# Storing the expert results from ScalarE's queue instead of SyncE's

## The chip, the cores and the metric

The kernel runs on one core of a Trainium2 chip. The metric is the device time of one execution in microseconds. The engines are TensorE (PE; its weight loads are PEld), VectorE (DVE), ScalarE (ACT), GpSimd (POOL) and SyncE (SP). SP computes nothing; its queue issues DMA transfers. In the profile a name such as L1021 is a line of the kernel, and `out<-in` are tile names with the buffer numbers left out.

## What is computed

Pooled attention for 4 batches and 8 heads, and on its result one feed-forward layer (the "experts" of the code) with an ELU between two matrix products:

```python
q_pool = q.reshape(B, H, S // 2, 2, D).mean(axis=3)        # (4, 8, 576, 64)
scores = scale * np.matmul(q_pool, k.transpose(0, 1, 3, 2)) # (4, 8, 576, 1152)
attn = softmax(scores)
x = np.matmul(attn, v)            # rearranged to (2304, 512)
h = x @ w_in                      # (2304, 2048)
g = np.where(h > 0, h, np.exp(np.minimum(h, 0)) - 1)
return g @ w_out                  # (2304, 512), float32
```

## The kernel before

Each batch is a unit of 576 pooled query rows. Inside a unit the heads go in four pairs, and each pair in nine steps of 128 query rows (the last step takes 64 rows of both heads). Every float32 operand is split into a high and a low float16 part, and products are summed from three terms.

One attention step is a fixed chain over engines: PE makes the scores (lines 721 and 730); DVE reads them from PSUM, scales them and finds the row maximum (line 736); ACT takes the exponential (line 742) and the row sum (line 747); DVE takes its reciprocal (line 750); ACT or POOL writes the high part of the probabilities (lines 761 and 753); DVE writes the low part (line 756); a transposing DMA from SP's queue turns `ep` into `pT` (line 780); PE multiplies it with v (lines 819 and 825); ACT and DVE join the two parts (lines 837 and 842). There are three `ep` buffers, so DVE's line 736 of a later step must wait until the transpose of the step three before has read its buffer.

The experts of a unit come in two groups of 256 and 320 rows and are interleaved with the attention of the next unit. The first product is line 933, with lines 941, 944, 949, 954, 968 and 972 behind it; the second is line 1000. Its result is evicted per tile of 128 rows by ACT (`oe`, line 1011) from PSUM into a `tmp` buffer in SBUF. The last tile of a unit has 64 rows only, whose two halves ACT (line 1013) and then DVE (line 1014) add. Then `od` (line 1021) stores the tile to `out`. That makes five stores a unit, 20 in all: 16 of 256 KB and four of 128 KB.

A planner written in Python sets the order of everything. Each piece of work is a task with an engine, an expected duration, a key and the tasks it depends on. The planner runs a clock over five engines, "DMA" among them, and whenever one is free it starts the ready task with the smallest key. `emit` then writes the tasks' instructions in the order in which the planner started them, so each engine's queue has a fixed order, and a queue does not pass an instruction that waits. A store is a DMA task that depends on its eviction; the planner's clock starts it when its DMA engine comes to it, which may be well after the eviction:

```python
toe = plan.add("ACT", 605.0, pos[0] - CFG["KO"], oe, [prev, txd2], [op, ot, us])
plan.add("DMA", Move(480.0, 480.0), pos[0], od, [toe], [ot])
```

All 372 transfers of the program before are issued from SP's queue: loads of q, k, v and the weights, the small copies of `qT`, the transposes and the stores. Completion is counted on eight semaphores, used in turn.

Of the kernel before, what the change touches and what calls it, by code (L numbers as in the profile page):

```python
# [226 lines left out]
def attention_moe_kernel(  # L227
# [9 lines left out]
    nc = tc.nc  # L237
# [131 lines left out]
    def w_out16(g):  # L369
        return w_out[g // 2].ap[:, 2 * (g % 2):2 * (g % 2) + 2]  # L370
# [485 lines left out]
    def experts(u, gi, t0, t1):  # L856
# [5 lines left out]
        def step(cost):  # L862
            at = pos[0]
            pos[0] += (t1 - t0) * cost / total
            return at
# [51 lines left out]
        if True:  # L917
# [72 lines left out]
            for o in range(0, n, 128):  # L990
                tn = min(128, n - o)
                op, ot = plan.buf("r"), plan.buf("tmp")
                prev = None
                for qd in range(4):
                    def m2(qd=qd, o=o, tn=tn, gt=gt, op=op):
                        for i12 in range(12):
                            fi, (a, e) = i12 // 3, ((0, 0), (0, 1), (1, 0))[i12 % 3]
                            f, i = qd * 4 + fi, qd * 12 + i12
                            r0 = 0 if tn == 128 else 64 * (i % 2)
                            nc.tensor.matmul(  # L1000
                                op.ap[r0:r0 + tn, :], gt[qd].ap[:, a, fi, o:o + tn], w_out16(f // 2)[:, e, f % 2, :],
                                start=(i < 128 // tn), stop=(i >= 48 - 128 // tn), skip_group_check=(tn < 128),
                            )

                    c = 12 * (216.0 if tn == 128 else 110.0)
                    deps = gdone[qd] + w_done[1][2 * qd] + w_done[1][2 * qd + 1] + [prev]
                    prev = plan.add("PE", c, step(c), m2, deps, [op, gt[qd], w_out[qd]])

                def oe(o=o, tn=tn, op=op, ot=ot):
                    if tn == 128:  # L1010
                        nc.scalar.activation(out=ot.ap, in_=op.ap, func=AF.Copy, scale=us.ap[:, 4:5])
                    else:
                        nc.scalar.activation(out=ot.ap[0:64], in_=op.ap[64:128], func=AF.Copy, scale=us.ap[0:64, 4:5])
                        nc.vector.scalar_tensor_tensor(
                            out=ot.ap[0:64], in0=op.ap[0:64], scalar=us.ap[0:64, 4:5], in1=ot.ap[0:64],
                            op0=ALU.mult, op1=ALU.add,
                        )

                def od(o=o, tn=tn, ot=ot, g0=g0):
                    r0 = u.b * SQ + u.s0 + g0 + o  # L1020
                    nc.sync.dma_start(out=out[r0:r0 + tn, :], in_=ot.ap[0:tn])  # L1021

                toe = plan.add("ACT", 605.0, pos[0] - CFG["KO"], oe, [prev, txd2], [op, ot, us])
                plan.add("DMA", Move(480.0, 480.0), pos[0], od, [toe], [ot])

    for u in units:
# [37 lines left out]
```

## Time and profile before

| | us |
|---|---|
| runs shown, median of 3 | 947.41 |
| runs shown, lowest and highest | 945.33, 953.8 |
| profiled execution, device time | 947.0 |
| profiled execution, span from the first to the last instruction | 945.2 |

The profile is one execution. A row of the timeline gives the start, the time taken, the engine (with a q when it is the engine's queue that issues or waits), the line, the operation, the tiles, how many instructions were merged, and in brackets how long the engine had stood idle and what ended that. Times are counted from the span's start. Issues of DMA transfers and waits on semaphores are work of a queue and don't count as busy time of an engine.

### The profile page before, as it was taken

The numbers are of one execution on the slowest core, as the hardware profiler recorded it, in microseconds if no ns is written. First come the engines' busy times: TensorE is split into PE (matmuls) and PEld (weight loads), VectorE is DVE, ScalarE is ACT, GpSimd is POOL, SyncE is SP. The second block draws the span as 40 slices with busy tenths as digits, with TensorE's granted clock in tenths as the row PEclk, the third lists the DMA queues.
The fourth block names the chain that finished last, engine by engine and source line by source line (L and its number), as shares of the span: only waits on it lengthen the run. The fifth ranks groups of instructions, "written<-read, shape, count | busy, mean of one in ns | idle before, by whom it ended". The sixth has DMA issues, their size and how long they took to land.

```text
span 945.2 us, 14736 instructions
## 1 busy us (share of the span) xinstructions
PE 740.6 (78%) x5283; PEld 420.6 (44%) x5283; DVE 728.4 (77%) x1235; ACT 691.2 (73%) x1169; POOL 370.6 (39%) x344
## 2 busy tenths in 40 slices
PE   0256555566939898988997989769979899789997
PEld 0123232233716455445644544338436544366563
DVE  5998999989898878867785897877877897785220
ACT  4587868878778879767777997568877987675360
POOL 3420513101737757402623772226324852034260
PEclk9998656657959999999998989989989999789999
DMA  7899999999948679897598989886799889754000
GB/s 235 221 211 199 232 224 250 237 188 263 224 95 182 133 166 207 153 185 125 110 186 183 196 172 208 160 160 105 158 212 202 170 157 173 133 100 76 23 1 28
DMA packets 434056, 156.94 MB, mean 166 GB/s; under 512 B 395840, under 2 KB 414272, under 8 KB 433984
## 3 DMA queue, kind: packets, MB, share of 16 engines
q1 hardware_dynamic: 433984, 156.01, 79.6%
q8 instruction: 41, 0.67, 0.3%
q14 instruction: 31, 0.25, 0.1%
HBM read 45.09 MB, written 4.72 MB: 53 GB/s over the span
## 4 chain that ended last, share of the span: by engine, by line
PE 28%; DVE 17%; DMA 14%; ACT 7%; issue 6%; POOL 5%; SPq 1%; DVEq 0%; POOLq 0%; ACTq 0%
DMA pT<-ep 11%; PE r L933 11%; PE r L1000 9%; DVE ep L736 6%; DVE ep L756 5%; PE r L819 3%; ACT ep L742 3%; PE s L721 2%; PE r L825 2%; POOL g L972 2%; PE s L730 1%; DMA kT<-kn 1%; DVE x L842 1%; ACT ep L761 1%; ACT tmp L944 1%
## 5 line engine op out<-in xcount | busy, mean ns | idle before, releaser
L756 DVE SCALAR_TENSOR_TENSOR ep<-ep,nm 128x1152 f16<-128x1152 f32 x132 | 209.7, 1593 | 18.1 <-ACT ep L761 10.5
L742 ACT ACTIVATE ep<-ep,nm 128x1152 f32<-128x1152 f32 x132 | 165.2, 1251 | 77.4 <-DVE ep L736 57.9
L736 DVE TENSOR_SCALAR_CACHE_REDUCE ep<-s,sm 128x1152 f32<-128x1152 f32 x132 | 186.3, 1411 | 40.6 <-DMA pT<-ep 25.7
L933 PE MATMUL r<-x,wi 128*128 128x256 f16 (+1 forms) x1536 | 204.1, 293 | 8.1 <-DVE x L842 4.2
L721 PE MATMUL s<-kT,qT 128*128 128x512 f16 (+3 forms) x480 | 108.8, 368 | 90.8 <-DVE ep L736 71.3
L933 PEld LDWEIGHTS <-wi 128*128 128x128 f16 x1536 | 150.5, 100 | 58.4 <-issue 18.3
L1000 PE MATMUL r<-wo,g 128*128 128x512 f16 (+1 forms) x864 | 174.4, 380 | 0.0
L761 ACT ACTIVATE ep<-ep,nm 128x1152 f16<-128x1152 f32 x111 | 138.3, 1247 | 23.7 <-DVE nm L750 23.3
L819 PE MATMUL r<-pT,v 128*128 128x256 f16 (+1 forms) x855 | 107.3, 281 | 31.1 <-DMA pT<-ep 16.5
L1000 PEld LDWEIGHTS <-g 128*128 128x128 f16 (+1 forms) x864 | 73.1, 100 | 87.9 <-issue 9.3
L949 POOL TENSOR_SCALAR tmp<-tmp,us 128x320 f32<-128x320 f32 (+1 forms) x96 | 73.2, 765 | 93.3 <-ACT tmp L944 92.9
L721 PEld LDWEIGHTS <-qT 128*128 128x128 f16 (+1 forms) x480 | 40.8, 105 | 144.5 <-issue 113.6
L819 PEld LDWEIGHTS <-v 128*128 128x128 f16 x864 | 72.5, 108 | 62.6 <-issue 33.1
L954 DVE SCALAR_TENSOR_TENSOR tmp<-r,wk,tmp 128x320 f32<-128x320 f32 (+1 forms) x96 | 57.5, 611 | 31.0 <-POOL tmp L949 30.6
L753 POOL TENSOR_SCALAR ep<-ep,nm 128x1152 f16<-128x1152 f32 x21 | 29.2, 1392 | 128.7 <-DVE nm L750 127.3
L972 POOL TENSOR_TENSOR g<-tmp,g 128x320 f16<-128x320 f32 (+1 forms) x70 | 72.1, 1036 | 12.0 <-ACT g L968 10.4
L730 PE MATMUL s<-kT,qT 64*128 64x512 f16 (+3 forms) x480 | 72.2, 369 | 0.0
L825 PE MATMUL r<-pT,v 128*64 128x256 f16 (+1 forms) x855 | 67.6, 282 | 0.0
L384 POOL TENSOR_SCALAR q<-q,sm 128x576 f32<-128x576 f32 x14 | 12.6, 897 | 134.6 <-ACT qn L429 119.2
L941 ACT ACTIVATE tmp<-r 128x320 f32<-128x320 f32 (+1 forms) x96 | 46.5, 485 | 24.4 <-PE r L933 19.6
L944 ACT ACTIVATE tmp<-tmp,us 128x320 f32<-128x320 f32 (+1 forms) x96 | 58.0, 608 | 1.3
L837 ACT ACTIVATE x<-r,sm 64x256 f32<-64x256 f32 (+1 forms) x96 | 39.8, 414 | 23.7 <-PE r L825 22.3
(123 smaller groups left out, 960.1 us busy)
## 6 DMA issues: line engine op xcount, KB each, us to landing
k<-in_k_dram SPq DMA_DIRECT2D x16, 576.0 KB, 5.0
v<-in_v_dram SPq DMA_DIRECT2D x16, 576.0 KB, 4.6
q<-in_q_dram SPq DMA_DIRECT2D x32, 256.0 KB, 3.4
qT<-qT SPq DMA_DIRECT2D x48, 144.0 KB, 2.8
g<-in_moe_w_in_dram SPq DMA_DIRECT2D x13, 512.0 KB, 5.6
g<-in_moe_w_out_dram SPq DMA_DIRECT2D x13, 512.0 KB, 5.2
out_dram<-tmp SPq DMA_DIRECT2D x16, 256.0 KB, 2.8
pT<-ep SPq DMA_TRANSPOSE x130, 4.8
```

What stands on the lines that cost most here:

```text
L721: nc.tensor.matmul(s.ap[rows, c, 0:n], pr.qT.ap[:, 0, j, rows], keys[h][c], start=True, stop=False, skip_group_check=True,)
L730: nc.tensor.matmul(s.ap[rows, c, 0:n], pr.qT.ap[r, 1, j, rows], keys[h][c][r], start=False, stop=True, skip_group_check=True,)
L736: nc.vector.tensor_scalar(e_(), s.ap.rearrange("p a b -> p (a b)")[:, 0:S], pr.sm.ap[:, 12:13], None, op0=ALU.mult, op1=ALU.min, accum_out ...
L742: nc.scalar.activation(out=e_(), in_=e_(), func=AF.Exp, bias=nm.ap[:, 0:1], scale=-1.0, accum_out=nm.ap[:, 2:3],)
L756: nc.vector.scalar_tensor_tensor(out=p_(1), in0=e_(), scalar=nm.ap[:, 3:4], in1=p_(0), op0=ALU.mult, op1=ALU.subtract)
L761: nc.scalar.activation(out=p_(0), in_=e_(), func=AF.Copy, scale=nm.ap[:, 3:4])
L819: nc.tensor.matmul(x.ap[:, os], vt[:, order[c]].rearrange("p e d -> p (e d)"), pT.ap[:, c, cs], start=(c == 0), stop=False, skip_group_che ...
L825: nc.tensor.matmul(x.ap[r0:r0 + 64, os], vt[:, order[c], 0], pT.ap[:, NCH + c, cs], start=False, stop=(c >= NCH - 2), skip_group_check=True,)
L933: nc.tensor.matmul(hp.ap[:, f * n:(f + 1) * n], w[:, a, c, (f0 + f) * 128:(f0 + f + 1) * 128], x16.ap[:, e, c, g0:g0 + n], start=(i == 0), ...
L949: nc.gpsimd.tensor_scalar(en.ap[:, :m], en.ap[:, :m], -1.0, us.ap[:, 5:6], op0=ALU.add, op1=ALU.mult)
L972: nc.gpsimd.tensor_tensor(out=l, in0=gv, in1=h, op=ALU.subtract)
L1000: nc.tensor.matmul(op.ap[r0:r0 + tn, :], gt[qd].ap[:, a, fi, o:o + tn], w_out16(f // 2)[:, e, f % 2, :], start=(i < 128 // tn), stop=(i >= ...
```

## The change

The function `od` issues the store from ScalarE's queue. The planner's tasks, keys and durations are the same, so the order in which instructions are emitted is the same too; the 20 stores leave SP's order and stand in ACT's order, at the place where they were emitted.

```diff
                 def od(o=o, tn=tn, ot=ot, g0=g0):
                     r0 = u.b * SQ + u.s0 + g0 + o
-                    nc.sync.dma_start(out=out[r0:r0 + tn, :], in_=ot.ap[0:tn])
+                    nc.scalar.dma_start(out=out[r0:r0 + tn, :], in_=ot.ap[0:tn])

                 toe = plan.add("ACT", 605.0, pos[0] - CFG["KO"], oe, [prev, txd2], [op, ot, us])
                 plan.add("DMA", Move(480.0, 480.0), pos[0], od, [toe], [ot])
```

## Rows read from the trace of the kernel before

**Rows 1.** The page, busy time, share and instructions of each engine.

```profile
PE 740.6 (78%) x5283; PEld 420.6 (44%) x5283; DVE 728.4 (77%) x1235; ACT 691.2 (73%) x1169; POOL 370.6 (39%) x344
```

**Rows 2.** The page, the chain that ended last: shares of the span by line.

```profile
DMA pT<-ep 11%; PE r L933 11%; PE r L1000 9%; DVE ep L736 6%; DVE ep L756 5%; PE r L819 3%; ACT ep L742 3%; PE s L721 2%; PE r L825 2%; POOL g L972 2%; PE s L730 1%; DMA kT<-kn 1%; DVE x L842 1%; ACT ep L761 1%; ACT tmp L944 1%
```

**Rows 3.** Line 1021: issue in ns (min/median/max), first and last start.

```profile
L1021 SPq DMA_DIRECT2D out_dram<-tmp x20: 332/536/1487, 338.2 to 941.8; - x20
```

**Rows 4.** SP's own waits: who waited for whom, total us, times, longest us.

```profile
SPq L1021 <- ACT tmp L1011: 69.1, 4, 44.9
```

**Rows 5.** Timeline of SP, 860 to the end.

```profile
858.51 7.06 SPq L780 DMA_TRANSPOSE pT<-ep  x2
879.54 62.74 SPq L1021 DMA_DIRECT2D out_dram<-tmp  x5
```

**Rows 6.** Line 780, the same view; then who waited for its landing (us, times).

```profile
L780 SPq DMA_TRANSPOSE pT<-ep x130: 2382/2846/5228, 52.5 to 862.7; - x130
...
  DVE ep L736: 26.2, 27
...
DMA to landing us min/median/max: 4.5/4.9/10.1
```

**Rows 7.** Timeline of SP around three stores of the body.

```profile
405.12 1.49 SPq L1021 DMA_DIRECT2D out_dram<-tmp  x1
406.71 3.31 SPq L780 DMA_TRANSPOSE pT<-ep  x1
...
581.91 4.10 SPq L780 DMA_TRANSPOSE pT<-ep  x1
586.06 0.57 SPq L1021 DMA_DIRECT2D out_dram<-tmp  x1
586.74 7.08 SPq L780 DMA_TRANSPOSE pT<-ep  x2
...
798.34 0.35 SPq L1021 DMA_DIRECT2D out_dram<-tmp  x1
798.81 7.54 SPq L780 DMA_TRANSPOSE pT<-ep  x2
```

**Rows 8.** Timeline of DVE, 576 to 594: the reader behind the store at 586.06.

```profile
592.33 1.42 DVE L736 TENSOR_SCALAR_CACHE_REDUCE ep<-s,sm 128x1152 f32<-128x1152 f32 x1 [0.93 <-DMA pT<-ep]
```

**Rows 9.** Line 1011 from 339 to 341: ACT's queue; ns, then first and last start.

```profile
L1011 ACTq EVENT_SEMAPHORE  x1: 17/17/17, 340.0 to 340.0; - x1
```

**Rows 10.** Timeline of ACT at four places where a store is emitted.

```profile
337.49 0.67 ACT L1011 ACTIVATE tmp<-r,us 128x512 f32<-128x512 f32 x1
...
339.36 1.25 ACT L742 ACTIVATE ep<-ep,nm 128x1152 f32<-128x1152 f32 x1 [1.02 <-DVE ep L736]
...
584.43 1.25 ACT L742 ACTIVATE ep<-ep,nm 128x1152 f32<-128x1152 f32 x1
...
586.08 1.16 ACT L424 ACTIVATE kn<-v 128x1152 f16<-128x1152 f32 x1 [0.31 <-DMA v<-in_v_dram]
...
616.78 0.29 ACT L747 ACTIVATE nm<-nm,wk 128x1 f32<-128x1 f32 x1
617.47 1.26 ACT L742 ACTIVATE ep<-ep,nm 128x1152 f32<-128x1152 f32 x1 [0.39 <-DVE ep L736]
...
620.01 1.25 ACT L742 ACTIVATE ep<-ep,nm 128x1152 f32<-128x1152 f32 x1 [0.87 <-DVE ep L736]
...
809.64 0.69 ACT L1013 ACTIVATE tmp<-r,us 64x512 f32<-64x512 f32 x1 [0.43 <-PE r L1000]
811.61 1.26 ACT L742 ACTIVATE ep<-ep,nm 128x1152 f32<-128x1152 f32 x1 [1.28 <-DVE ep L736]
...
812.99 0.29 ACT L747 ACTIVATE nm<-nm,wk 128x1 f32<-128x1 f32 x1
```

**Rows 11.** Timeline of DVE, 807 to 817: the 64-row tile and line 747's reader.

```profile
811.49 0.74 DVE L1014 SCALAR_TENSOR_TENSOR tmp<-r,us,tmp 64x512 f32<-64x512 f32 x1
...
815.01 0.16 DVE L750 RECIPROCAL nm<-nm 128x1 f32<-128x1 f32 x1
```

## The prediction

> **What bounds the kernel now.** I read the busy shares first: PE 78%, DVE 77%, ACT 73% of the span [rows 1]. No engine is full, so what counts is who waits for whom. The chain that ended last says the same: its largest single item, 11%, is the transposing transfer `pT<-ep` (line 780), and the next are matmuls and the two big DVE passes [rows 2]. All those transfers are issued from SP's queue, in the order in which the planner wrote them, and the 20 stores of line 1021 stand in the same queue.
>
> So the question has two halves: what does SP's queue lose to the stores, and what will ACT's queue lose to them? A store occupies SP for 0.332 to 1.487 us, median 0.536 [rows 3]. The view of SP's own waits gives the largest number that speaks for the change: SP stood 69.1 us at line 1021 for the eviction of line 1011 [rows 4]. But it counts four waits, the longest 44.9 us, and the timeline of SP's end shows where they are: from 879.54 to the end SP holds five stores and nothing else [rows 5]. The transposes end before that. Nothing stands behind these waits, so removing them is worth nothing.
>
> **What is removed from SP.** Fifteen stores lie in the body (338 to 813 us), five in the tail. A body store delays something only where the next transfer was ready and had to go behind it. That is so in six spots; the first is 405.12 to 406.71 (1.59 us), the last 798.34 to 798.81 (0.47) [rows 7]; the four between them are 0.70, 0.71, 2.16 (two stores together) and 0.68. In sum 6.3 us of SP's time. In the other spots SP's next transfer waits for something else anyway.
>
> Of those six, I followed each transfer to its first reader. Only where the reader stands idle for the landing can an earlier issue count. It does at 586.06: SP's transpose ends at 586.01, the store takes 586.06 to 586.63, the next transpose starts at 586.74 [rows 7]; DVE's line 736 then sits idle 0.93 us until that transfer lands and starts at 592.33 [rows 8]. The chain runs through this piece too. Without the store the transpose starts 0.68 us earlier and DVE can use all of it, since 0.93 is more. At 405.12 the reader is held by PE at the same moment, and at 798.81 DVE gains at most half a microsecond, which the next landing takes back. I take -0.7 us, with 0 and -6.3 as the ends.
>
> **What is added to ACT: the place.** The planner fixes each engine's order, and the change doesn't alter it. So a store's place in ACT's order is where the planner emits it: behind ACT instructions that it started earlier, often several after the eviction. I read the places off the emitted order of the program before. ACT's sequencer works ahead of its engine: the semaphore wait for an eviction ran at 340.0 [rows 9] while the engine was still in the exponential that started at 339.36 and takes 1.25 us [rows 10]. So issuing a store need not stop the engine; it is hidden as long as it ends before the next ACT instruction may start anyway.
>
> **What is added to ACT: the cost.** No row shows a transfer issued from ACT. The nearest are the same store on SP, 0.332 to 1.487 us [rows 3], and, far off, a transpose, median 2.846 [rows 6]. I take the median 0.536, since it is the same transfer in size and shape, and keep 0.332 and 2.846 as ends. The cover is the time from where ACT's sequencer reaches the store to the start of the next ACT instruction. It has twelve values in the body (three pairs of stores stand together): the first is 338.16 to 339.36, 1.20 us [rows 10]; then 1.01, 1.37, 1.38, 1.97, 3.32 (a pair), 1.55, 0.69 (a pair), 1.25 (a pair), 0.52, 1.26; the last is negative, below. At 0.536 a store only three are too short:
>
> - The pair behind line 747 at 616.78: two stores end at 617.86, line 742 started at 617.47, so it is 0.39 late. The ACT instruction after it, 620.01, had 0.87 us of idle time [rows 10]. Absorbed: 0.
> - One store with 0.52 of cover is 0.02 late. 0.
> - The store of the 64-row tile. It needs DVE's line 1014, which ends at 812.23 [rows 11], and it stands right behind line 1013 (809.64) and ahead of line 742 (811.61) [rows 10]. This is the one new wait that the change makes: line 742 would start at 812.23 + 0.54 = 812.77, 1.16 us late. Late next is line 747, at 814.15 in place of 812.99, done at about 814.4. Its reader is DVE's line 750, which runs at 815.01 behind another DVE pass [rows 11]. Absorbed with 0.6 us to spare: 0. If that cover were gone it would cost 1.2 us.
>
> Each DMA also waits for the one eight issues back to land (eight completion counters are used in turn). The eight issues before a body store span well over its landing time, at worst 10.1 us for a transpose [rows 6], so I cost this wait at 0. Nobody in the trace waits for a store to land, so nothing is gained by freeing `tmp` sooner.
>
> In the tail the ACT instructions stand 2 to 15 us apart, and the last store follows DVE's line 1014 as before: 0, with -0.2 to +1.0 if its issue takes 0.33 or 1.49 in place of its 0.50.
>
> **Sum.** 947.0 (the profiled execution: span 945.2 and 1.8 around it) - 0.7 + 0 = 946.3 us. That execution is 0.4 below the median 947.41 of the three runs shown, which spread from 945.33 to 953.8.
>
> **Rivals.**
>
> *A shared generator (slightly slower).* ACT's store may have to wait while SP is issuing a transpose, which keeps SP 2.4 to 5.2 us [rows 6]. In before only one queue issues, so no row shows it. Five body stores would meet one: for instance SP's transpose of 581.91 runs to 586.01 [rows 7], so the store behind line 742 (584.43) would end at 586.55 and line 424 (586.08) [rows 10] would be 0.5 late. The other four give 0.1, 0.5, 0.7 and 0.1; with the 1.2 and 0.4 above, 3.5 us if all of it passed on, and SP's gain is lost: at most 950.5. The Trainium skill (Perfetto Trace Analysis, DMA Instruction - HWDGE) says that the descriptor generator is shared by two sequencers and locked for exclusive use; that is this rival, and by it the time would be between 947 and 950.5 in place of 946.3. No run so far shows it.
>
> *The issue holds ACT long (the other side: slower).* If a store kept ACT as long as a transpose keeps SP, 2.85 us, all twelve covers would be too short, by 27.9 us together. If all passed on: 975; if a third did, as ACT's gaps absorb the rest: 956. It decides (over 1%) from about 1.6 us a store if everything passes on. Against it: the same store takes 0.54 on SP, and the covers were followed by idle ACT time in most spots.
>
> *SP was the bound (faster).* If all 6.3 us counted: 940.7. For it: 11% of the chain is these transfers [rows 2], and DVE's line 736 sat idle 26.2 us for them in 27 waits [rows 6]. Against it: five of the six readers were held by something else.
>
> That the change doesn't take hold can't be: one line emits all 20 stores.
>
> **How the numbers follow.** Forecast (little moves, within 2 us of 946.3): 0.66. Shared generator, 947 to 950.5: 0.17. SP was the bound, near 941 to 944: 0.08. ACT held long, 952 and up: 0.09. The range 942.5 to 952 takes in the forecast, the shared generator and the spread of the runs, and leaves out the outer parts of the other two. One per cent is 9.5 us, about what a measurement of this kernel can tell from no change. Only the long hold reaches it on the slow side (0.08 of its 0.09), and on the fast side nothing I priced does: 6.3 is 0.7%; I leave 0.03 for it. Same: 0.89.
>
> **What would show it.** Line 1021 as 20 issues on ACT's queue near 0.54 us each: right; medians above 1.6 speak for the long hold, and long issues only where SP is in a transpose speak for the shared generator. The transpose after 586.0 should follow its predecessor at once, and DVE's idle time before line 736 there shrink by 0.7. Line 742 near 812 should start about 1.2 us late and line 750 at 815 not move. ACT's busy time must stay at 691 us. I am wrong if ACT's idle time ahead of lines 742 and 761 grows by over 10 us, or if the transposes land clearly sooner throughout.

## The result and the profile after

The changed kernel is slower: 956.0 us, median of nine runs (952.18 to 962.48), against 950.48 us for the kernel before on the same chip (942.96 to 953.8). The ratio is 1.0075, 95% interval 1.0047 to 1.0102, about 7 us (the two medians alone are 5.5 us apart). That is within the 1% that the prediction called no change, but it is a loss and not nothing. The forecast was 946.3 us with a range up to 952.0, so the range does not hold the result. Part of the miss is the level: the forecast started from one execution of 947.0 us, 3.5 below the median of the kernel before in this measurement. The rest is the change: -0.7 forecast, +5.5 between the medians.

The page of the changed kernel (span 952.3, device time 954.04): busy time of the engines, the DMA queues, and two groups with their idle time.

```profile
PE 739.6 (78%) x5283; PEld 418.7 (44%) x5283; DVE 726.3 (76%) x1235; ACT 690.8 (73%) x1169; POOL 371.1 (39%) x344
...
q1 hardware_dynamic: 431360, 151.29, 78.4%
q10 hardware_dynamic: 2624, 4.72, 1.5%
...
L742 ACT ACTIVATE ep<-ep,nm 128x1152 f32<-128x1152 f32 x132 | 165.2, 1251 | 85.8 <-DVE ep L736 61.4
L736 DVE TENSOR_SCALAR_CACHE_REDUCE ep<-s,sm 128x1152 f32<-128x1152 f32 x132 | 186.3, 1412 | 49.4 <-DMA pT<-ep 33.9
```

No engine works noticeably longer than in [rows 1]: POOL 0.5 us more, the others less, ACT by 0.4. The 20 stores now have a DMA queue of their own, q10, and idle time has grown: ahead of ACT's line 742 by 8.4 us, which waits mostly for DVE's line 736, and ahead of line 736 itself, where DVE stands 49.4 us. That row before:

```profile
L736 DVE TENSOR_SCALAR_CACHE_REDUCE ep<-s,sm 128x1152 f32<-128x1152 f32 x132 | 186.3, 1411 | 40.6 <-DMA pT<-ep 25.7
```

So 8.2 of the 8.8 us of new idle time there are waits for the landing of transposes (33.9 against 25.7). One profile can mislead here: the second profile of the changed kernel, below, has 40.6 us in all as before, 29.2 of them for transposes. Line 1021 after (issue in ns, then the landing in us) and line 780 after (issue, who waited for the landing, landing):

```profile
L1021 ACTq DMA_DIRECT2D out_dram<-tmp x20: 338/339/538, 342.2 to 948.9; - x20
...
DMA to landing us min/median/max: 2.0/2.7/5.1
```

```profile
L780 SPq DMA_TRANSPOSE pT<-ep x130: 2398/2830/5402, 53.4 to 869.9; - x130
...
  DVE ep L736: 34.6, 25
  PE r L819: 25.5, 19
...
DMA to landing us min/median/max: 4.5/5.1/10.2
```

Issuing on ACT is cheap, 0.339 us in the middle; [rows 3] had 0.536 on SP. The transposes land no sooner although their queue has lost 20 transfers: the median is 5.1 us in place of 4.9 in [rows 6], and line 736 waits 34.6 us for them in place of 26.2 (this view counts a little more than the page's row).

### The profile page after: what moved, and what is told of

It reads as the page before. It is cut to its first block, busy times and chain, and to the rows that moved or that the text cites. A ratio compares the mean times of both kernels' runs of the same rounds, so it can differ in the third digit from the quotient of the medians.

```text
span 952.3 us, 14730 instructions
## 1 busy us (share of the span) xinstructions
PE 739.6 (78%) x5283; PEld 418.7 (44%) x5283; DVE 726.3 (76%) x1235; ACT 690.8 (73%) x1169; POOL 371.1 (39%) x344
## 5 line engine op out<-in xcount | busy, mean ns | idle before, releaser
L736 DVE TENSOR_SCALAR_CACHE_REDUCE ep<-s,sm 128x1152 f32<-128x1152 f32 x132 | 186.3, 1412 | 49.4 <-DMA pT<-ep 33.9
L756 DVE SCALAR_TENSOR_TENSOR ep<-ep,nm 128x1152 f16<-128x1152 f32 x132 | 205.8, 1564 | 18.1 <-ACT ep L761 10.4
L761 ACT ACTIVATE ep<-ep,nm 128x1152 f16<-128x1152 f32 x111 | 138.3, 1248 | 23.3 <-DVE nm L750 23.1
L819 PE MATMUL r<-pT,v 128*128 128x256 f16 (+1 forms) x855 | 104.9, 276 | 34.0 <-DMA pT<-ep 21.0
L753 POOL TENSOR_SCALAR ep<-ep,nm 128x1152 f16<-128x1152 f32 x21 | 29.2, 1392 | 131.9 <-DVE nm L750 130.6
L972 POOL TENSOR_TENSOR g<-tmp,g 128x320 f16<-128x320 f32 (+1 forms) x70 | 69.0, 992 | 13.7 <-ACT g L968 12.1
```

What stands on the lines that cost most here:

```text
L736: nc.vector.tensor_scalar(e_(), s.ap.rearrange("p a b -> p (a b)")[:, 0:S], pr.sm.ap[:, 12:13], None, op0=ALU.mult, op1=ALU.min, accum_out ...
L756: nc.vector.scalar_tensor_tensor(out=p_(1), in0=e_(), scalar=nm.ap[:, 3:4], in1=p_(0), op0=ALU.mult, op1=ALU.subtract)
L761: nc.scalar.activation(out=p_(0), in_=e_(), func=AF.Copy, scale=nm.ap[:, 3:4])
L819: nc.tensor.matmul(x.ap[:, os], vt[:, order[c]].rearrange("p e d -> p (e d)"), pT.ap[:, c, cs], start=(c == 0), stop=False, skip_group_che ...
L972: nc.gpsimd.tensor_tensor(out=l, in0=gv, in1=h, op=ALU.subtract)
```

## The spot where the gain was forecast

This is SP of the changed kernel around the store that SP issued at 586.06 before, the spot of the forecast gain; its rows before are in [rows 7].

```profile
581.38 3.42 SPq L780 DMA_TRANSPOSE pT<-ep  x1
584.89 0.54 SPq L473 DMA_DIRECT2D v<-in_v_dram  x1
585.49 13.78 SPq L780 DMA_TRANSPOSE pT<-ep  x3
...
589.94 3.33 SPq L780 DMA_TRANSPOSE pT<-ep  x1
```

And ACT of the changed kernel at that moment:

```profile
588.24 1.26 ACT L742 ACTIVATE ep<-ep,nm 128x1152 f32<-128x1152 f32 x1 [0.49 <-DVE ep L736]
588.57 0.34 ACTq L1021 DMA_DIRECT2D out_dram<-tmp  x1
```

The gap of 0.73 us between two transposes on SP (586.01 to 586.74 in [rows 7]) is gone: the transpose of 585.49 takes 4.36 us to issue and the next stands at 589.94. The store left ACT at 588.57, while SP was still issuing the transpose of 585.49, and took 0.34 us. Now DVE behind it, first in the kernel before (its row of 592.33 is in [rows 8]), then in the changed kernel:

```profile
588.21 1.42 DVE L736 TENSOR_SCALAR_CACHE_REDUCE ep<-s,sm 128x1152 f32<-128x1152 f32 x1 [0.49 <-DMA pT<-ep]
```

```profile
593.37 1.42 DVE L736 TENSOR_SCALAR_CACHE_REDUCE ep<-s,sm 128x1152 f32<-128x1152 f32 x1 [1.76 <-DMA pT<-ep]
...
596.68 1.42 DVE L736 TENSOR_SCALAR_CACHE_REDUCE ep<-s,sm 128x1152 f32<-128x1152 f32 x1
```

The 0.93 us of idle time of [rows 8] is gone at 596.68, as forecast. But one line 736 earlier, 1.27 us are lost (0.49 to 1.76). That instruction waits for the transpose *ahead* of the store, the one of 581.91 in [rows 7] and of 585.49 after. Line 780 cut to this one transfer, in the kernel before and in the changed kernel:

```profile
L780 SPq DMA_TRANSPOSE pT<-ep x1: 4096/4096/4096, 581.9 to 581.9; - x1
...
DMA to landing us min/median/max: 6.2/6.2/6.2
```

```profile
L780 SPq DMA_TRANSPOSE pT<-ep x1: 4364/4364/4364, 585.5 to 585.5; - x1
...
DMA to landing us min/median/max: 7.7/7.7/7.7
```

The store came 4.15 us after that transpose's start before (586.06 - 581.91), behind it in the same queue. It comes 3.08 us after it now (588.57 - 585.49), in another queue, and the transpose lands 1.5 us later.

So the vanished idle time cannot be put down to the transpose that leaves SP sooner: a DVE that comes 1.27 us later loses no 0.93 us to it anyway. The idle time is just as gone in two kernels, described below, in which SP still issues this store and the transpose ahead of it landed late for another reason or beside another store (ACT's waits, then the whole extra stores):

```profile
593.84 1.42 DVE L737 TENSOR_SCALAR_CACHE_REDUCE ep<-s,sm 128x1152 f32<-128x1152 f32 x1
```

```profile
599.98 1.42 DVE L736 TENSOR_SCALAR_CACHE_REDUCE ep<-s,sm 128x1152 f32<-128x1152 f32 x1
```

The forecast itself is borne out where the store is left out and the transpose ahead lands as before, after 6.2 us: in the kernel without body stores the two lines 736 start 3.31 us apart, against 4.12 before.

## The theories

Four ways to lose 7 us were put against each other.

- *Collision*: a store in a queue of its own no longer stands behind the transpose in flight but shares the DMA engines with it, and that transpose lands later.
- *ACT's order*: ACT waits at the new place for evictions (above all for DVE's line 1014), or the issue holds it.
- *A second queue* slows every transfer, or the start of the program.
- *Noise*: the two profiles differ by accident. There was reason to suspect it: at the first store, at 338 us, the changed kernel already lagged by 4.0 us, and up to there the two programs do the same.

## The experiments

**The two kernels again.** Both unchanged.

> The kernel before, unchanged, against itself. All theories: ratio 1.000 within 0.003. It gives a second profile of before: how far do two profiles of one program drift apart by the time of the first store (before against the changed kernel: 4.0 us at 338 us)? Theory 'noise': its DVE instruction that stood at 342.3 us lies elsewhere by up to 4 us, in either direction. Theory 'second queue': it lies within 1 us of 342.3, because the program is the same.

> The changed kernel, unchanged, for a second profile of it. All theories: ratio 1.005 to 1.010. Theory 'collision' (a store from ACT runs beside a transpose in flight and makes it land later): the landings of the transposes beside the stores are again 0.4 to 1.6 us later than in before at the same places, and the place of the DVE instruction at 342.3 us is noise. Theory 'second queue' (two issuing queues slow all transfers): that instruction is 3 to 5 us late again.

The kernel before against itself gave 1.0011 (0.9985 to 1.0037), the change 1.0077 (1.0044 to 1.0110). The loss is real. The lag of 4.0 us at 338 us is not part of it: the repeated kernel before stands 3.35 us behind its own first profile at the same DVE instruction. One execution against another shifts by some microseconds, and only averages over several profiles, or a place where all of one kind agree, can be read.

**Which stores?** Only the last unit's five stores on ACT, or only the body's 15:

```diff
-                    nc.sync.dma_start(out=out[r0:r0 + tn, :], in_=ot.ap[0:tn])
+                    q_ = nc.scalar if u.i == B - 1 else nc.sync      # the tail; the body: u.i < B - 1
+                    q_.dma_start(out=out[r0:r0 + tn, :], in_=ot.ap[0:tn])
```

> Only the five stores of the last unit are issued from ACT, the fifteen of the body from SP. No transpose is in flight beside those five. Collision: ratio 1.000 within 0.003. Second queue: the program uses two issuing queues, so 1.004 to 1.008, with the lag there before the first store. ACT hold (ACT's order waits for the store): 1.000, since ACT is idle there.

> The fifteen stores of the body from ACT, the five of the last unit from SP. Collision: the whole loss, ratio 1.005 to 1.010. Second queue: the same. ACT hold: the same. If it is 1.000, the tail or noise made the loss, and all three fall.

The tail gave 1.0014 (0.9983 to 1.0044), the body 1.0093 (1.0063 to 1.0124). The loss is made by the 15 stores of the body; a second queue as such slows nothing that these runs can measure. The stretches of the kernel before show what is different there (the last columns are PE's granted clock, the DMA engines' busy share and GB/s):

```profile
337.00:820.00 483.00, 424.98 (x3161) 242.70 (x3159) 377.89 (x619) 373.62 (x623) 206.60 (x198) 0.95 0.86 168
820.00:945.00 125.00, 116.25 (x822) 70.64 (x821) 50.05 (x88) 61.26 (x112) 39.48 (x48) 0.94 0.25 51
```

In the body the DMA engines are busy 86% of the time, in the tail 25%, and in the tail no transpose is in flight any more ([rows 5]).

**How many bytes?** Each store takes 16 of the 512 columns, on ACT and on SP; the rest of the output is not written.

```diff
-                    nc.sync.dma_start(out=out[r0:r0 + tn, :], in_=ot.ap[0:tn])
+                    nc.scalar.dma_start(out=out[r0:r0 + tn, 0:16], in_=ot.ap[0:tn, 0:16])   # and with nc.sync
```

> All 20 stores from ACT at the same places in its order and with the same waits, but each moves only 16 of the 512 columns (64 bytes a row in place of 2 KB); the other columns of the output are not written. Collision of data (the store's bytes share the DMA engines with the transpose in flight): the loss goes, ratio 0.997 to 1.002; the transpose that starts near 582 lands about 6.2 us after its issue as in before, not 7.3 to 7.7. Generator or ACT's order (the issue itself, its waits, or the new wait on line 1014 cost the time): the loss stays, 1.005 to 1.010.

> The control: the same thin stores (16 of 512 columns, the rest of the output not written) from SP, as in before. Both theories: 0.997 to 1.001. If it is as much below 1 as the thin stores on ACT are below the changed kernel, then it is the bytes alone, on whichever queue; collision says that only ACT's queue gains much from thin stores, 5 to 8 us against at most 2 here.

On ACT 1.0025 (0.9997 to 1.0052), on SP 0.9980 (0.9954 to 1.0006). Most of the loss goes with the bytes. Between the two thin kernels a difference of 0.45% remains, with intervals that only just overlap, so a part may not be bytes: 128 packets a store are left. One expectation failed: with the thin stores on ACT the transpose of 582.80 still landed after 7.2 us, not after about 6.2. The reason is given with the run on ACT's waits.

**Twice the bytes, and none.** Each tile stored also to a spare buffer from ACT; and the body's stores left out.

```diff
-                    nc.sync.dma_start(out=out[r0:r0 + tn, :], in_=ot.ap[0:tn])
+                    nc.scalar.dma_start(out=out[r0:r0 + tn, :], in_=ot.ap[0:tn])
+                    spare = dr.tile([128, DM], F32, name=f"spare{r0}")
+                    nc.scalar.dma_start(out=spare[0:tn, :], in_=ot.ap[0:tn])
```

```diff
-                    nc.sync.dma_start(out=out[r0:r0 + tn, :], in_=ot.ap[0:tn])
+                    if u.i == B - 1:
+                        nc.sync.dma_start(out=out[r0:r0 + tn, :], in_=ot.ap[0:tn])
```

> The changed kernel with every tile stored twice from ACT, the second time into a spare buffer in HBM: double bytes and double issues. Collision of data: the loss about doubles, ratio 1.011 to 1.018, and the transpose near 582 lands 8 us or more after its issue. Generator or ACT's order: each store adds only its 0.34 us on ACT, mostly covered: 1.007 to 1.011.

> The fifteen stores of the body are left out (those rows of the output are not written), the last five stay on SP. What the stores cost before at most. By the prediction's sum (SP loses at most 6.3 us to them, 0.7 of it on the path): 0.997 to 1.000; if SP was the bound: 0.993 to 0.995.

Twice gave 1.0108 (1.0056 to 1.0161): the interval is too wide to tell twice the loss from the same loss, and the transpose near 582 landed after 7.9 us, just short of the 8 that collision asked for. Without the body's stores the ratio is 0.9968 (0.9942 to 0.9995): a better place for them can bring about 3 us, by the interval 5.5 at most.

**One store alone.** Only the store of the spot above goes to ACT.

```diff
-                    nc.sync.dma_start(out=out[r0:r0 + tn, :], in_=ot.ap[0:tn])
+                    q_ = nc.scalar if (u.i, g0, o) == (1, 256, 0) else nc.sync
+                    q_.dma_start(out=out[r0:r0 + tn, :], in_=ot.ap[0:tn])
```

> Only one of the 20 stores (second unit, row 256 of it, the one that SP issued at 586.06 us before) goes to ACT's queue; the others stay on SP. Collision (a store that no longer queues behind the transpose in flight makes that transpose land later): the transpose issued about 581.9 lands after 7.2 to 7.8 us in place of 6.15 to 6.25, and DVE's line 736 behind it at 588.2 is idle for 1.4 to 1.9 us in place of about 0.5, although nothing else in the program differs. ACT's order or an accumulated shift (the late landing there is an effect of the stores ahead of it): the transpose lands after 6.15 to 6.25 us as in the kernels whose stores are all on SP. The total of one store can't be told from no change (under 0.1%).

Line 780 cut to the transpose ahead of that store, and the line 736 behind it on DVE's timeline:

```profile
L780 SPq DMA_TRANSPOSE pT<-ep x1: 4433/4433/4433, 587.2 to 587.2; - x1
...
DMA to landing us min/median/max: 7.0/7.0/7.0
```

```profile
594.38 1.42 DVE L736 TENSOR_SCALAR_CACHE_REDUCE ep<-s,sm 128x1152 f32<-128x1152 f32 x1 [1.42 <-DMA pT<-ep]
```

A landing after 7.0 us and 1.42 us of idle time, just short of the late landing that collision asked for (7.2) and at the low end of its idle time; the store does it without its 19 siblings. One reservation belongs here, and it comes from the run with ACT's waits below: with every store on SP, that execution also had a landing of 7.5 us at this place. The spot alone therefore proves little; the totals must, and the landings of all transposes taken together.

**Not the 64-row tiles.** The 16 stores of 128 rows on ACT, the four that need line 1014 on SP.

```diff
-                    nc.sync.dma_start(out=out[r0:r0 + tn, :], in_=ot.ap[0:tn])
+                    q_ = nc.scalar if tn == 128 else nc.sync
+                    q_.dma_start(out=out[r0:r0 + tn, :], in_=ot.ap[0:tn])
```

> The 16 stores of 128 rows go to ACT's queue, the four of 64 rows, the only ones whose store makes ACT wait for DVE's line 1014, stay on SP. Collision: 1.006 to 1.009, as with all 20 on ACT (1.0077). The new wait of ACT for line 1014: 1.000 to 1.003, and the full change's loss comes back with the three 64-row tiles of the body.

It gave 1.0068 (1.0035 to 1.0101): the loss stays without the new wait.

**Another engine's queue.** The body's stores from GpSimd's queue.

```diff
-                    nc.sync.dma_start(out=out[r0:r0 + tn, :], in_=ot.ap[0:tn])
+                    q_ = nc.gpsimd if u.i < B - 1 else nc.sync
+                    q_.dma_start(out=out[r0:r0 + tn, :], in_=ot.ap[0:tn])
```

> The 15 stores of the body are issued from GpSimd's queue, at the same place of the emitted order; the last unit's five stay on SP. Collision (any queue that isn't SP's lets the store go beside the transpose): 1.005 to 1.010, as with ACT (1.0093), and the transpose issued about 581.9 lands after 7.2 to 7.8 us in place of 6.2. ACT's order, or an issue that holds ACT: 0.997 to 1.002, ACT's order being that of the kernel before, and the transpose lands after 6.2 us. POOL's own order may add a wait of POOL's instructions for an eviction; it would show as idle time ahead of lines 753 and 972.

It gave 1.0082 (1.0053 to 1.0112), with ACT's queue exactly as before the change. The page of that kernel, the queue of the stores and line 736, and line 780 cut to the transpose ahead of the store of 586.06:

```profile
q0 software_dynamic: 1104, 3.54, 1.1%
...
L736 DVE TENSOR_SCALAR_CACHE_REDUCE ep<-s,sm 128x1152 f32<-128x1152 f32 x132 | 186.4, 1412 | 43.8 <-DMA pT<-ep 28.6
```

```profile
L780 SPq DMA_TRANSPOSE pT<-ep x1: 4061/4061/4061, 587.3 to 587.3; - x1
...
DMA to landing us min/median/max: 7.1/7.1/7.1
```

The landing of 7.1 us is again just short of the 7.2 that collision asked for. POOL now waits 46 us in all for evictions at the stores, but its idle time ahead of lines 753 and 972, where a cost of its order was to show, has not grown (95.5 and 12.0 us, against 128.7 and 12.0 before). So the loss comes without any change in ACT's order or ACT's issues.

**ACT's waits without the transfers.** All stores on SP; at the same place of ACT's order a copy of one column of the tile.

```diff
                     nc.sync.dma_start(out=out[r0:r0 + tn, :], in_=ot.ap[0:tn])
+                    if u.i < B - 1:
+                        nc.scalar.activation(out=touch[0:tn, 0:1], in_=ot.ap[0:tn, 511:512], func=AF.Copy)
```

> All stores are issued from SP as before; where the change puts one of the 15 body stores into ACT's order there stands instead a copy of one column of the tile (128x1) on ACT, so ACT waits there for the same eviction (and for DVE's line 1014 at the 64-row tiles) and loses a short instruction, but no transfer leaves SP's queue. Collision: 0.998 to 1.003, and the transpose issued about 581.9 lands after 6.2 us. ACT's order (what the place in ACT's queue costs): 1.005 to 1.010 and line 742 at 811.6 idle for about 3 us as in the changed kernel.

It gave 0.9979 (0.9951 to 1.0008). ACT's timeline of this kernel at the 64-row tile (the added line moves the numbers of those below by one, so 1014 is the eviction and 1015 DVE's addition):

```profile
811.33 0.69 ACT L1014 ACTIVATE tmp<-r,us 64x512 f32<-64x512 f32 x1 [0.43 <-PE r L1001]
813.84 0.20 ACT L1024 ACTIVATE touch<-tmp 64x1 f32<-64x1 f32 x1 [1.83 <-DVE tmp L1015]
813.95 1.24 ACT L743 ACTIVATE ep<-ep,nm 128x1152 f32<-128x1152 f32 x1
```

The wait is made here, and 15 instructions besides, and it costs nothing that can be measured. ACT's order falls.

What made the transpose at the spot land after 7.5 us here, with no store beside it? The DMA view also lists transfers of the kind "instruction", 8 KB or 16 KB each. While that transpose is in flight (582.85 to 590.39) it shows one:

```profile
q14 instruction: 1, 0.01, 0.3%
```

The same view shows one such transfer beside the transpose in the changed kernel (both profiles), with the body's stores, the whole tiles or the thin stores on ACT, and none in the kernel before (both profiles), with the tail on ACT, with the body on GpSimd or with the one store on ACT. So at this spot two causes are mixed: a landing after 6.2 us with neither, 7.0 and 7.1 with the store alone, 7.5 with the instruction transfer alone, 7.3 to 7.7 with both. The edits moved that transfer in time, and it can account for the late landing beside the thin stores.

**The stores stay, and a second one comes beside them.** What was left open is whether SP's transposes, leaving sooner, crowd each other. Here SP keeps everything, and ACT stores each body tile once more, whole or 16 columns of it:

```diff
                     nc.sync.dma_start(out=out[r0:r0 + tn, :], in_=ot.ap[0:tn])
+                    if u.i < B - 1:
+                        spare = dr.tile([128, DM], F32, name=f"spare{r0}")
+                        nc.scalar.dma_start(out=spare[0:tn, :], in_=ot.ap[0:tn])      # thin: [0:tn, 0:16] on both
```

> All 20 stores are issued from SP as before; beside each of the 15 body stores ACT issues a second store of the same tile (256 KB) to a spare buffer in HBM, at the place the change uses. The output is the reference's; the spare stores are extra work. Collision (a store in a queue of its own goes beside the transpose in flight): 1.005 to 1.012, as with the stores moved, although SP's queue keeps all it had. The loss comes from SP (its transposes leave sooner and crowd each other once the stores are gone from its queue): 0.998 to 1.003.

> As the run with extra stores, but the extra store takes 16 of 512 columns (8 KB): the issue on ACT, the wait for the eviction and 128 descriptors stay, 31 of 32 bytes go. Collision through the bytes: 0.999 to 1.003. Collision through the issue or the descriptors of a second queue: 1.005 or more, near the run with full extra stores.

Whole gave 1.0106 (1.0063 to 1.0150), thin 1.0035 (1.0003 to 1.0068). The page of the kernel with whole extra stores, and its line 1024:

```profile
q10 hardware_dynamic: 1968, 3.54, 1.1%
...
L736 DVE TENSOR_SCALAR_CACHE_REDUCE ep<-s,sm 128x1152 f32<-128x1152 f32 x132 | 186.3, 1412 | 49.0 <-DMA pT<-ep 34.6
```

```profile
L1024 ACTq DMA_DIRECT2D spare<-tmp x15: 321/327/560, 344.6 to 823.6; - x15
...
DMA to landing us min/median/max: 2.1/4.0/6.3
```

15 stores that nobody waits for, issued in 0.327 us each, cost 10 us, and line 736's waits for transposes rise from 25.7 to 34.6 as with the change. SP's transposes need not leave sooner for it. The 10 us hold the bytes as well as their queue: the same second stores issued from SP weren't run. Leaving the body's stores out on SP saves 3 us; if as many bytes more on SP cost as much, about 7 of the 10 are left for the queue (an estimate).

## Where the 7 us are

All kernels whose stores are whole and single run the same DVE instructions in the same order, so their starts can be compared one by one. Four profiles have the body's stores on SP (the kernel before twice, the tail on ACT, ACT's waits), five have them elsewhere (the change twice, body on ACT, whole tiles on ACT, body on GpSimd). Between the first store and 941 us the mean of the five falls 5.2 us behind the mean of the four. The single profiles scatter: against that mean the five lose 6.0, 1.4, 8.4, 5.3 and 5.1 us, the four 2.9, -0.4, -4.4 and 1.9. By stretches (times of the kernel before):

| stretch | SP's stores in it before | us lost, mean of 5 against mean of 4 |
|---|---|---|
| 396 to 412 | 405.12 | +0.96 |
| 490 to 511 | two, 498.65 and 499.34 | +1.01 |
| 580 to 590 | 586.06 | +1.23 |
| 590 to 597 | none, the forecast gain's place | -0.01 |
| 700 to 791 | 702.80, 703.43, 787.04 | +1.76 |
| 791 to 804 | 798.34 | +0.50 |
| 804 to 815 | 812.26, the 64-row tile | +0.57 |
| all others together | | -0.8 |

The row of 490 to 511 shows no loss by itself: it rests on one of the four profiles, 2.88 us ahead, while the other three lie among the five.

The waits of line 736 for transposes tell the same in one number per profile: 25.7, 27.0, 24.7 and 28.2 us with the body's stores on SP (mean 26.4), and 33.9, 29.2, 35.3, 31.5 and 28.6 elsewhere (mean 31.7). The difference is 5.3 us. A single profile is a weak witness: the kernel with two stores a tile, at 1.0108, shows 28.7. At the spot above, the transpose ahead of the store landed after 6.2, 6.2, 6.2 and 7.5 us in the four, and after 7.7, 7.3, 7.4, 7.6 and 7.1 in the five. The one at 400.57 landed after 7.8, 7.3, 7.3 and 7.3 against 8.4, 8.7, 8.7, 8.4 and 7.2; the one at 795.13 after 4.7 to 4.8 in all four against 6.3, 4.9, 6.3, 6.1 and 4.7.

All transposes together say it more firmly. Take the 94 issued after 338 us in each of the five profiles, each against the mean landing of the same transpose in the four. In 65 cases at least 16 packets of a store from another queue start while the transpose is in flight: these land 0.47 us later in the mean (95% interval 0.32 to 0.63). The other 405 land 0.03 us earlier. Beside thin stores on ACT (11 cases) the difference is -0.20 us, with 0.36 either way: no lateness is seen without the bytes. 65 cases in five profiles at 0.47 us are 6.1 us of later landing in one execution, and not all of it is waited for. Instruction transfers go with late landings too, whoever holds the stores: 13 transposes had one beside them in some of the four profiles only, and landed 0.58 us later there (0.26 to 0.89).

How large can it be? The changed kernel's DMA view from 585 to 595 gives the store's queue 7.4% of the 16 engines over 10 us:

```profile
q1 hardware_dynamic: 5848, 1.99, 99.8%
q10 hardware_dynamic: 144, 0.26, 7.4%
```

That is 0.74 us of the engines' time, in a stretch in which the other queue's packets fill them already (the two shares add up to more than 100%, so packets overlap in this record). The 15 body stores, three of them half as large, come to about 10 us in this way, an estimate of the size and no bound: the transpose at the spot landed 0.8 us later beside a store alone.

Three things stay open. In 804 to 815 all of the change's 0.57 us also show in the thin stores on SP and in the kernel without body stores, so that stretch is not explained by the collision. And what the thin stores still cost on ACT (1.0025 and 1.0035, against 0.998 on SP) may be the issue or chance; the intervals don't settle it, and late landings beside them are not seen. How a DMA engine orders the packets of two queues isn't shown, as the trace doesn't name the engine of a packet. It is not that the store's packets run earlier: at the spot they run from 5.38 to 6.40 us after the transpose's issue in the kernel before, which landed after 6.15, and from 5.35 to 6.24 with the one store on ACT, where it landed after 6.99. A store on ACT that is held back until no transpose is in flight wasn't tried: ACT would have to wait for the landing, which changes more than the store.

## Why the prediction was wrong, point by point

- **What is removed from SP.** This step failed. It asked who stands *behind* a store in SP's queue and found six spots, and one that counts, 586.06; there the idle time went as forecast in both profiles of the changed kernel (0.8 us against the shift), but by luck: DVE had just been held up for longer, and the same idle time went where SP kept the store. In the three others with the body's stores off SP it did not go (DVE then waited for PE), so that the mean of the stretch 590 to 597 is 0. It did not ask who stands *ahead*. A transpose in flight lands later beside a store from another queue, 0.47 us in the mean of 65 cases, than with that store behind it in its own queue. The missing term is about 0.8 us at that spot (the store alone, 7.0 and 7.1 us against 6.2), as much as the 0.7 hoped for, and 5 to 7 us in all. It was priced at nothing, since the sum had only sequencers and engines in it and not the 16 DMA engines, though a view of the stretches would have shown their busy share, 86% in the body.
- **The ends of that step.** "SP was the bound" allowed -6.3 us. Leaving the body's stores out altogether gives 0.9968, some 3 us, and the interval ends at 5.5 us, so that rival falls. What a better place for the stores could bring is small: no kernel here beats the one before by more than its measurement is uncertain, apart from that one.
- **The cost of an issue on ACT.** Taken as 0.536, it measured 0.339 (0.338 to 0.538), at the lower bound of 0.332. "The issue holds ACT long" falls, although its time with a third passed on, 956, is what was measured: that is a coincidence.
- **The new wait at the 64-row tile.** Right in place and size, in this profile. The changed kernel's ACT, then its DVE:

```profile
819.17 0.49 ACTq L1021 DMA_DIRECT2D out_dram<-tmp  x1
819.71 1.25 ACT L742 ACTIVATE ep<-ep,nm 128x1152 f32<-128x1152 f32 x1 [3.26 <-DVE tmp L1014]
```

```profile
818.40 0.74 DVE L1014 SCALAR_TENSOR_TENSOR tmp<-r,us,tmp 64x512 f32<-64x512 f32 x1
...
821.92 0.16 DVE L750 RECIPROCAL nm<-nm 128x1 f32<-128x1 f32 x1
```

  Against [rows 10, 11] line 1014 starts 6.91 us later, line 742 8.10, line 750 6.91: line 742 is 1.19 us late beyond the shift (1.16 forecast) and line 750 not at all. The run without that wait confirms that it costs nothing that can be measured (1.0068 against 1.0077).
- **The shared generator.** The store at 588.57 ran in 0.34 us while SP was in the transpose of 585.49 to 589.85. By the lock that the Trainium skill describes (Perfetto Trace Analysis, DMA Instruction - HWDGE) it would have lasted to the end of that transpose; the row shows nothing of it. Of the six stores that ACT issued in the changed kernel while SP was in a transpose, five took 0.338 to 0.343 us and one 0.538; the other 14 took 0.338 to 0.502. This rival had the sign right, and its mechanism is the wrong one.
- **The tail at 0.** 1.0014 with the tail alone on ACT: right as far as it can be measured.
- **What would show it.** ACT's idle time ahead of line 742 grew by 8.4 us and ahead of line 761 by none (23.7 to 23.3); the mark was 10. The idle time at line 736 shrank by the forecast amount, and that sign said "right" where the mechanism was another. The test that would have told, transposes landing *later*, was not on the list.

The Trainium skill has a rule for what was missed (DMA: Bandwidth & Descriptors, Queues, rings and completion order): each DMA engine takes turns between the queues for which it has work, a packet at a time. The landings fit it, 0.47 us later in the mean of the 65 transposes beside a store from another queue; the turns themselves no row here shows. Another section of that page (Issuing engines are not separate DMA queues) says that issuing from several engines saves only time on the sequencer; here that time was worth nothing that the total shows, and the second queue had a price.

## What to carry to other kernels

A queue is also an order of service: moving a transfer that nobody waits for out of a queue of transfers that somebody waits for lets it compete with them. So look not only at who stands behind a transfer but at what is in flight ahead of it, at who waits for that, and at the busy share of the DMA engines in that stretch: at 86% the move cost 0.75%; at 25%, with no transpose in flight, nothing that could be measured. And a queue's sequencer that looks blocked for long (69.1 us in the waits) may have nothing behind it that matters. Look also at the transfers of kind "instruction": an edit moves them, and one of them beside a transfer can look like the effect that is sought.

## What was not expected of the hardware

- A store issued from ACT takes 0.339 us and one from GpSimd 0.587, the same store from SP 0.536 in the middle; in the changed kernel five of the six that ACT issued while SP was issuing a transpose took 0.34 us.
- A transfer of 256 KB that nobody waits for, issued from a second queue, made the transposes in flight beside it land 0.47 us later in the mean (65 cases), and 15 such stores, three of them of 128 KB, cost about 7 us of 950.
- A transfer of kind "instruction" of 8 or 16 KB in flight beside a transpose went with a landing 0.58 us later (13 transposes), at the spot 7.5 us in place of 6.2.
- Two executions of one unchanged kernel stood 3.35 us apart at 338 us, with equal spans at the end (945.2 and 945.2).
